# A new list of operations for a gated recurrence followed by a highway layer

## The chip, the cores and the metric

The kernel runs on one core of one Trainium2 chip. The metric is device microseconds of one execution. Of three runs of the kernel before, the median is 208.43 us (207.93 to 208.6).

One core has five engines with instruction streams of their own: TensorE (PE, matrix products and transposes; its weight loads are shown as PEld), VectorE (DVE), ScalarE (ACT), GpSimd (POOL) and SyncE (SP, which here issues the DMA transfers). Each works through its stream in order; between engines semaphores make an instruction wait for its data or for a buffer.

## The reference, cut to what matters

```python
# x, f_logit: [4, 6336, 256] float32; lower_bound: [256]; w_h, w_t: [256, 256]; b_t: [256]
sig = 1.0 / (1.0 + np.exp(-f_logit))
f = lower_bound + (1.0 - lower_bound) * sig
i = 1.0 - f
h = np.zeros((B, D))
for t in range(S):                      # a recurrence along the 6336 tokens of each sequence
    h = f[:, t] * h + i[:, t] * x[:, t]
    y[:, t] = h

y = y.reshape(B * S, D)                 # 25344 tokens of 256 channels
H = np.maximum(y @ w_h, 0.0)
T = 1.0 / (1.0 + np.exp(-(y @ w_t + b_t)))
out = T * H + (1.0 - T) * y             # float32
```

## The kernel before, in words

The 25344 tokens are cut into 28 units, numbered 0 to 27: two of 256 tokens, one of 512, twenty-three of 1024, one of 512 and one of 256. The recurrence runs along the tokens, so for it the data are turned: channels on the 128 partitions, in two halves (h = 0 and 1), tokens along the free axis.

A unit goes through these operations. The letter is the name in the list; the number behind it is the unit, and what stands behind the dot is the half or the piece.

| name | engine | what it does | line |
|---|---|---|---|
| l, x | SP | load of f_logit and of x for the unit (1 MB each for 1024 tokens) | L244 |
| u | ACT | u = sigmoid(-f_logit) | L256 |
| b | POOL, or DVE with a "v" | bv = u * x, in pieces of 512 tokens | L264 |
| i | PE | transposes of u, one half, into a PSUM bank (slots 0 and 1: a0, a1) | L271 |
| f | ACT, or DVE with a "v" | f = 1 + ncc * uT, one half | L282, L280 |
| p | PE | transposes of bv, one half, into a0 or a1 | L291 |
| s | DVE | the recurrence itself, a scan along the tokens, one half | L308 |
| z, g | PE | products of y with w_t and with w_h, for one half of the outputs | L320, L114 |
| t | ACT | t = sigmoid(z + b_t) | L333 |
| d | DVE | d = max(g, ncc * y), which with the folded weights is relu(y w_h) - y | L337 |
| e | POOL, or DVE with a "v" | d = d * t, in pieces | L343 |
| o | PE | back to tokens on partitions, and y + d added up in PSUM | L365, L366 |
| c | ACT, or DVE with a "v" | copy of o from PSUM to SBUF | L378, L376 |
| w | SP | store | L382 |

y is kept without the factor (1 - lower_bound), which is folded into the weights (WT, WH) and into the diagonal matrix that o uses (dg). cc and ncc are that factor and its negative. They come from lower_bound, transposed on PE by pc; pb and cb do the same for b_t. wt and wh load the weights. The token k is not part of the computation: k*3 puts three matmuls of zeros on PE, into the PSUM slot named behind it.

The order of everything is a list written out by hand or by a planner, one token for each operation, run from left to right (`for token in order.split()`). Each token issues its instructions, and every instruction is pinned (`tc.keep_in_program_order`), so the list fixes the order on each engine's stream. SP's stream too: a store whose copy isn't done holds back the loads behind it, and a load waits until the buffer that it names is free. The number behind the colon is the buffer: l and x have six slots each (0 to 5), u, f, bv and o four; z, g and o share three PSUM slots of two banks (0, 1, 2), and i and p two of one bank (a0, a1), which at the start and the end other operations use as well.

One more rule stands in the code (`shared`): a product on POOL (b, e) waits for the last product on DVE, or for the last of WT, WH and dg, that stands ahead of it in the list.

Of the kernel before, what the change touches and what calls it, by code (L numbers as in the profile page):

```python
# [53 lines left out]
e1.1 e1.0 k*2:0 w0.0 u4:1 z2.0:1 f3.0:1 z2.1:0 b4.0:1 s3.1:0 p3.0:0 o1.0:2 t2.1:0 u27:0 b4.1 c1.0:1 s3.0 w1.0 x8:3
i4.0:1 g2.0:0 f4.0:0 d2.0 i4.1:1 p4.0:0 l9:1 x9:4 l11:4 t2.0 u5:2 e2.1v e2.0v z3.0:0 g3.1:1 b27.0:0 z3.1:2 s4.0:1
p4.1:0 f4.1:1 i5.0:1 t3.0:0 t3.1 d3.1:1 b5.0:2 g3.0:0 f5.0:0 s4.1 o2.0:1 u6:1 b5.1 c2.0:2 d3.0 w2.0 i5.1:1 x11:0 e3.2
g4.1:2 p5.0:0 d4.1:0 b6.0:1 f5.1:1 s5.0:2 z4.1:0 t4.1:1 p5.1:1 b6.1 u7:2 e3.1 s5.1 l10:0 z4.0:1 t4.0 g4.0:0 i6.0:0
e3.0v p6.0:1 d4.0 o3.0:1 e4.2 b7.0:2 f6.0:0 s6.0:3 e4.0v i6.1:0 b7.1 u8:3 f6.1:1 o3.1:0 c3.0:0 c3.1:1 w3.1 w3.0 g5.0:2
p6.1:0 i8.1:1 z5.0:1 f8.1:0 x10:1 e4.1 t5.0:0 g5.1:0 i7.1:1 b8.0:1 s6.1 i7.0:0 d5.0:1 z5.1:1 l12:2 f7.1:1 p7.1:1 d5.1
f7.0:2 t5.1 b8.1 g6.0:2 p7.0:0 e5.1 k*3:0 o4.1:1 s7.1:0 z6.0:0 d6.0:2 s7.0 u9:1 b9.0:2 g6.1:2 c4.1:3 d6.1 i9.0:1  # L60
t6.0:1 b9.1 o4.0:1 u11:2 i9.1:0 f9.0v:1 c4.0:2 w4.0 e6.0v f9.1:2 g7.1:0 z6.1:2 k*3:1 e5.2v i8.0:1 z7.0:1 e5.0v t6.1
w4.1 f8.0:3 p8.1:0 d7.1:0 t7.0:0 g7.0:2 e6.1 p8.0:1 b11.0:3 o5.0:0 u10:1 c5.0:0 w5.0 x12:2 o5.1:1 c5.1:1 w5.1 s8.1:1
i11.1:0 z7.1:0 f11.1:0 s8.0 b11.1 l13:0 d7.0 p9.0:1 i10.1:0 z8.0:1 e6.2 b10.1:1 g8.1:2 t7.1 f10.1:3 p9.1:0 s9.0:2
o6.1:0 x13:0 i10.0:1 d8.1:1 s9.1 g8.0:2 t8.0:1 u12:3 o6.0:1 f10.0:1 c6.1:0 c6.0:2 b10.0 e7.0 i11.0:1 w6.0 p10.0:0 w6.1
f11.0:2 z8.1:0 t8.1 z9.0:1 t9.0:0 d8.0 g9.0:2 s10.0:3 i12.0:1 p10.1:0 l14:1 f12.0:1 d9.0:2 o7.0:0 g9.1:1 c7.0:1 x14:1
w7.0 s10.1 u13:1 o7.1:2 c7.1:3 w7.1 b12.0:2 l17:0 p11.0:1 d9.1 s11.0:0 z9.1:0 t9.1 i12.1:0 b12.1 l15:2 z10.1:1 g10.1:2
e8.0 t10.1:2 e9.0v b13.0:1 z10.0:0 f12.1:2 p11.1:1 b13.1 t10.0 o8.1:1 d10.1:0 p12.1:0 c8.1:0 o8.0:2 s11.1 u14:2
g10.0:0 d10.0 c8.0:2 b14.1:3 i13.1:1 e10.0 f13.1:0 g11.1:1 b14.0 z11.1:0 s12.1:1 d11.1:1 w8.0 t11.1:0 x15:0 w8.1
z11.0:2 i13.0:1 p12.0:0 s12.0 o9.0:0 t11.0 f13.0:2 g11.0:1 d11.0 o9.1:2 e11.0 p13.0:1 c9.0:1 u17:1 i14.0:0 f14.0v:1
c9.1:3 g12.0:0 u15:3 d12.0:2 b15.1:2 w9.0 z12.1:1 i17.0:0 f17.0:3 t12.1:1 o10.0:2 s13.0:2 o10.1:0 p13.1:0 c10.0:0  # L70
s13.1 b15.0 c10.1:1 i14.1:1 g12.1:1 z12.0:2 g13.0:0 i15.0:0 l16:1 f14.1:2 d12.1 p14.0:1 x16:2 d13.0:0 t12.0 o11.0:1
w9.1 g13.1:2 s14.0:3 f15.0:0 p14.1:0 o11.1:0 e12.0 w10.0 w10.1 i15.1:1 c11.0:2 u16:2 x17:1 b16.1:1 b16.0 z13.0:1 d13.1
f15.1:1 c11.1:0 z13.1:2 s14.1 t13.1:0 l18:0 t13.0 w11.0 p15.0:1 o12.1:0 i16.0:0 g14.1:2 s15.0:0 d14.1:1 e13.0 o12.0:1
p15.1:1 s15.1 c12.1:1 b17.1:2 f16.0:2 z14.1:0 z14.0:2 p16.0:0 s16.0:1 c12.0:3 t14.1:1 t14.0 g14.0:1 d14.0 i16.1:1
w11.1 l19:1 u18:3 x18:0 b17.0 e14.0 g15.1:0 d15.1:2 z15.0:2 i17.1:0 x19:3 f16.1:0 b18.0:3 p16.1:1 f17.1:1 b18.1 l20:2
s16.1 o13.1:1 t15.0:0 p17.0:0 g15.0:0 w12.1 d15.0 c13.1:0 u19:1 b19.1:1 o13.0:2 p17.1:1 z15.1:1 c13.0:2 z16.0:0
s17.1:2 t15.1 t16.0:1 z16.1:2 s17.0 g16.0:1 w13.1 t16.1 i18.0:1 d16.0:0 g16.1:0 o14.0:2 i18.1:0 f18.0:0 d16.1 e15.0v
o14.1:1 p18.0:1 s18.0:3 u20:2 w12.0 z17.0:0 c14.0:0 c14.1:1 f18.1:1 g17.0:2 d17.0:1 z17.1:1 b19.0 t17.0:0 i19.1:0
f19.1:0 p18.1:1 o15.1:0 w13.0 s18.1 t17.1 x20:1 i19.0:0 l21:0 g17.1:2 e16.0 d17.1 o15.0:1 f19.0:2 b20.0:2 b20.1
p19.1:0 x21:2 w14.0 i20.1:1 c15.1:2 g18.1:0 w14.1 s19.1:0 c15.0:3 z18.0:1 f20.1:1 l22:1 o16.0:2 d18.1:2 w15.1 u21:1  # L80
t18.0:1 p19.0:0 c16.0:0 i20.0:1 g18.0:0 s19.0 f20.0:0 o16.1:1 c16.1:1 z18.1:2 i21.1:0 b21.1:1 p20.0:1 t18.1 e17.0v
d18.0 o17.0:1 w15.0 z19.1:0 b21.0 f21.1:2 g19.0:2 s20.0:1 x22:0 d19.0:0 p20.1:0 s20.1 c17.0:2 t19.1:0 o17.1:1 u22:2
e18.0 z19.0:0 g19.1:2 b22.1:2 c17.1:3 t19.0 i21.0:1 d19.1 e19.0 i22.0:0 b22.0 f21.0:0 g20.1:1 z20.1:0 l23:2 w16.0
f22.0v:1 d20.1:1 w16.1 w17.0 x23:1 p21.1:1 w17.1 l24:0 u23:1 b23.0:3 t20.1:1 o18.0:2 o18.1:1 c18.0:0 s21.1:2 c18.1:1
p21.0:0 z20.0:0 b23.1 g20.0:2 i22.1:1 x24:2 t20.0 s21.0 f22.1:2 o19.1:1 p22.1:0 d20.0 c19.1:2 e20.0 i23.1:1 z21.0:0
g21.1:1 f23.1:0 t21.0:0 u24:2 p22.0:1 g21.0:2 b24.0:1 s22.1:3 i23.0:0 d21.1:2 f23.0:2 o19.0:0 z21.1:1 b24.1 s22.0
p23.1:0 d21.0 c19.0:3 t21.1 i24.0:1 w18.1 z22.0:0 z22.1:2 g22.1:1 s23.1:0 e21.0 w18.0 f24.0:1 w19.1 d22.1:0 l25:1
i24.1:1 x25:0 t22.0:1 t22.1 f24.1:0 e22.1 p23.0:0 o20.0:0 c20.0:0 w19.0 g22.0:1 p24.1:1 o20.1:2 u25:1 b25.0:2 s23.0
b25.1 p24.0:0 c20.1:1 d22.0 z23.0:0 s24.0:1 g23.0:1 t23.0:2 e22.0 l26:0 o21.0:2 c21.0:2 o21.1:0 s24.1 i25.1:0 g23.1:2
c21.1:3 x26:1 e22.2 g24.1:0 d23.0:1 f25.1:1 u26:2 b26.0:1 i27.1:1 i25.0:0 f27.1:0 d23.1 w20.0 z23.1:1 p25.0:1 f25.0:2  # L90
d24.1:2 s25.0:2 z24.0:2 p25.1:0 b26.1 t23.1 o22.0:0 e23.1 o22.1:1 t24.0:0 e23.2 z24.1:2 c22.0:0 s25.1 w20.1 g24.0:0
d24.0 e23.0v w21.0 c22.1:1 t24.1 w21.1 e24.0 w22.0 i26.0:1 e24.1 z25.0:1 i27.0:0 f26.0:2 g25.0:2 e24.2 i26.1:1 d25.0:0
# [330 lines left out]
```

## Time and profile before

| | |
|---|---|
| runs | 208.6, 207.93, 208.43 us |
| profiled execution, span from first to last instruction | 206.1 us |
| busy: PE, DVE, ACT, POOL | 192.6, 194.5, 191.9, 173.8 us |
| DMA, mean over the span | 78.68 MB, 382 GB/s |
| granted TensorE clock, mean | 0.995 |
| DVE waiting, longest | 4.4 us for the first load of x |
| SP waiting for copies of ACT ahead of stores | 110.2 us, 37 times |

Busy time is the union of an engine's instructions; the span counts from the first instruction of the program to the last, and a run takes 2 us more than it. PE's busy time counts matmuls in a pipeline and doesn't say that PE works at its peak.

### The profile page before, as it was taken

What the parts mean: (1) busy time and instruction counts of PE and PEld (TensorE: products, weight loads), DVE (VectorE), ACT (ScalarE), POOL (GpSimd) and SP (SyncE); (2) the same over time, 40 slices, a digit from 0 to 9 for tenths busy, and PEclk for the clock granted to TensorE, in tenths of its full rate; (3) what the DMA queues carried; (4) which work ended last, traced back from release to release, by engine and by line L of the source; (5) the groups of instructions that cost most, each with busy time, mean ns of one, the idle gap of its engine ahead of it and who ended that gap; (6) DMA issues with size and microseconds to landing.
All of it is one profiled execution on the core that took longest, in us unless ns stands there. A gap on an engine that the chain in (4) does not pass through costs nothing.

```text
span 206.1 us, 4635 instructions
## 1 busy us (share of the span) xinstructions
PE 192.6 (93%) x1837; PEld 133.8 (65%) x1837; DVE 194.5 (94%) x159; ACT 191.9 (93%) x192; POOL 173.8 (84%) x93
## 2 busy tenths in 40 slices
...
GB/s 196 370 424 422 411 418 423 409 423 417 414 423 408 429 417 426 423 420 413 425 424 416 433 411 417 429 415 418 407 422 422 414 392 378 286 104 204 138 382 248
DMA packets 16125, 78.68 MB, mean 382 GB/s; under 512 B 1764, under 2 KB 2536, under 8 KB 10216
## 3 DMA queue, kind: packets, MB, share of 16 engines
...
q8 instruction: 14, 0.23, 0.4%
...
q10 hardware_dynamic: 8, 0.00, 0.0%
...
## 4 chain that ended last, share of the span: by engine, by line
PE 53%; ACT 14%; DMA 13%; DVE 10%; issue 6%; POOL 2%; SPq 1%; ACTq 0%; DVEq 0%; POOLq 0%
DMA x<-in_x_dram 9%; DVE y L308 8%; PE op L366 7%; PE bT L291 7%; PE op L365 7%; PE g L320 7%; PE z L320 6%; PE uT L271 6%; PE g L114 6%; PE z L114 6%; ACT o L378 4%; ACT f L282 4%; DMA out_dram<-o 4%; ACT t L333 3%; POOL bv L264 2%
## 5 line engine op out<-in xcount | busy, mean ns | idle before, releaser
L264 POOL TENSOR_TENSOR bv<-u,x 128x1024 bf16<-128x1024 f16 (+1 forms) x49 | 100.9, 2085 | 16.9 <-DVE bt L207 10.7
L308 DVE TENSOR_TENSOR_SCAN y<-f,y,bT 128x1024 bf16<-128x1024 f16 (+5 forms) x54 | 106.8, 1989 | 0.2 <-PE bT L291 0.2
L343 POOL TENSOR_TENSOR d<-d,t 128x512 bf16<-128x512 bf16 (+3 forms) x33 | 73.3, 2234 | 9.6 <-DVE d L343 4.2
L337 DVE SCALAR_TENSOR_TENSOR d<-y,ncc,g 128x1024 bf16<-128x1024 bf16 (+2 forms) x56 | 63.1, 1137 | 1.5 <-PE g L320 1.0
L333 ACT ACTIVATE t<-z,bt 128x1024 bf16<-128x1024 f32 (+2 forms) x56 | 58.9, 1088 | 1.3 <-PE z L114 0.7
L282 ACT ACTIVATE f<-uT,ncc 128x1024 f16<-128x1024 f16 (+2 forms) x51 | 55.4, 1098 | 3.4 <-PE uT L271 2.2
L378 ACT COPY o<-op 128x1024 f32<-128x1024 f32 (+2 forms) x55 | 52.1, 984 | 2.4 <-PE op L366 1.6
L256 ACT ACTIVATE u<-l 128x2048 f16<-128x2048 f32 (+2 forms) x28 | 49.8, 1781 | 2.8 <-DMA l<-in_f_logit_dram 2.7
L366 PE MATMUL op<-ident_b,d 128*128 128x128 bf16 x396 | 49.5, 219 | 0.6 <-DVE d L343 0.6
L365 PE MATMUL op<-diag,y 128*128 128x128 f16 x396 | 49.7, 219 | 0.1
L366 PEld LDWEIGHTS <-d 128*128 128x128 bf16 x396 | 44.0, 113 | 3.2 <-DVE d L343 0.7
L365 PEld LDWEIGHTS <-y 128*128 128x128 bf16 x396 | 44.2, 113 | 1.7
L320 PE MATMUL g<-y,w_sb 128*128 128x512 bf16 (+1 forms) x112 | 39.5, 367 | 0.9 <-DVE d L337 0.7
L320 PE MATMUL z<-y,w_sb 128*128 128x512 bf16 (+1 forms) x112 | 39.3, 367 | 0.4 <-ACT o L378 0.4
L291 PE MATMUL bT<-ident_f,bv 128*128 128x128 f32 x198 | 31.8, 277 | 4.3 <-DVE y L308 2.6
L114 PE MATMUL z<-y,w_sb 128*128 128x512 bf16 x92 | 34.9, 379 | 0.0
L114 PE MATMUL g<-y,w_sb 128*128 128x512 bf16 x92 | 34.9, 379 | 0.0
L320 PEld LDWEIGHTS <-w_sb 128*128 128x128 f16 x224 | 21.6, 98 | 17.5 <-issue 0.9
L271 PEld LDWEIGHTS <-u 128*128 128x128 f16 x396 | 26.3, 98 | 10.2 <-issue 2.6
L271 PE MATMUL uT<-ident_h,u 128*128 128x128 f16 x396 | 31.2, 220 | 1.6 <-DVE y L308 0.8
L291 PEld LDWEIGHTS bT<-ident_f,bv 128*128 128x128 f32 x198 | 22.4, 141 | 12.3 <-ACT f L282 3.0
L114 PEld LDWEIGHTS <-w_sb 128*128 128x128 f16 x184 | 18.0, 98 | 16.7 <-issue 1.8
...
## 6 DMA issues: line engine op xcount, KB each, us to landing
...
l<-in_f_logit_dram SPq DMA_DIRECT2D x23, 1024.0 KB, 12.0
...
```

What stands on the lines that cost most here:

```text
L114: return pe.add_instruction(mybir.InstMatmult(name=nc.get_next_instruction_name(), start_tensor_calc=start, stop_tensor_calc=stop, tile_si ...
L264: shared(pin(e.tensor_mul(st[n]["bv"][:, a:c].rearrange("p k d j -> p k j d"), st[n]["u"][:, 2 * a:2 * c].rearrange("p (k j) d -> p k j d" ...
L271: pin(nc.tensor.transpose(uT[:, j * P:(j + 1) * P], st[n]["u"][:, j, h * P:(h + 1) * P], ident_h))
L282: pin(nc.scalar.activation(to, of, AF.Identity, scale=ncc[:, h:h + 1], bias=1.0))
L291: pin(nc.tensor.transpose(words[:, k:k + g * (P - 1) + 1:g], pair, ident_f))
L308: pin(nc.vector.tensor_tensor_scan(y[:, c:e], st[n]["f", h][:, c:e], st[n]["bT", h][:, c:e], 0.0 if fresh else carry[h], op0=ALU.mult, op1 ...
L320: pin(nc.tensor.matmul(p[:, a:e], w, half(n, "y", ki)[:, a:e], start=ki == 0, stop=ki == NH - 1))
L333: pin(nc.scalar.activation(half(n, "t", m), st[n]["z", m][:, :tokens(n)], AF.Sigmoid, bias=bt[:, m:m + 1]))
L337: pin(nc.vector.scalar_tensor_tensor(half(n, "d", m), half(n, "y", m), ncc[:, m:m + 1], st[n]["g", m][:, :tokens(n)], op0=ALU.mult, op1=AL ...
L343: shared(pin(e.tensor_mul(st[n]["d"][:, a:c], st[n]["d"][:, a:c], st[n]["t"][:, a:c])), not eng)
L365: pin(nc.tensor.matmul(o, half(n, "y", h)[:, cols], diag[:, h], start=True, stop=False))
L366: pin(nc.tensor.matmul(o, half(n, "d", h)[:, cols], ident_b, start=False, stop=True))
```

## The change

The list is replaced. Units, sizes of the pieces, buffers and the code of every operation stay as they are, word for word; the new file is two lines shorter, so its line numbers are lower by two behind the list. The new list has 822 tokens instead of 821.

What differs beside the order: which slot an operation names; which of the operations that can run on two engines run on DVE; and the idle matmuls' places. On DVE stand (b, e, f, c with a "v")

- before: b0.0 b1.0 b2.1 b3.1, e0.0 e2.1 e2.0 e3.0 e4.0 e6.0 e5.2 e5.0 e9.0 e15.0 e17.0 e23.0 e25.0 e25.2 e26.1 e27.1, f0.0 f1.1 f9.0 f14.0 f22.0, c25.1 c27.0
- after: b0.0 b1.0 b2.1 b3.0 b4.1, e1.0 e1.1 e0.0 e0.1 e2.1 e2.0 e3.2 e4.1 e5.2 e6.0 e6.2 e9.0 e15.0 e17.0 e23.1 e24.1 e25.2 e26.1 e27.1, f9.0 f14.0 f22.0, c25.0 c26.1 c27.0

The order on SP, at the start and in two later places:

```
before: l1 l0 x0 x1 l2 wt wh x2 l3 x3 l4 x4 l27 l5 x27 x5 l6 x6 l7 l8 x7 w0.0 w1.0 x8 l9 x9 l11 ...
after:  l0 x0 l1 wh l2 x1 x2 wt l3 x3 l4 l5 x4 x5 l6 l7 x6 l9 x9 x7 l8 w1.0 x8 w3.1 l10 w0.0 x10 ...
before: ... w6.0 w6.1 l14 x14 w7.0 w7.1 l17 l15 ... w11.0 w11.1 l19 x18 x19 l20 w12.1 w13.1 w12.0 w13.0 x20 ...
after:  ... x12 x14 w7.0 l14 w6.0 w6.1 l17 ... w12.0 l19 l27 w12.1 x27 w11.0 x18 x19 w10.0 w13.0 l20 ...
```

The diff, its first and last lines:

```diff
     order = """
-l1:0 l0:1 x0:0 x1:1 k*3:a0 l2:2 wt wh x2:2 l3:3 x3:3 l4:4 pc:0 x4:4 u0:0 l27:1 l5:5 b0.0v:0 x27:0 x5:5 u1:1 cc l6:0
-k*3:1 i0.1:0 f0.1:0 dg i1.0:1 b1.0v:1 f1.0:1 k*3:1 k*3:a0 p0.1:1 s0.1:0 i0.0:0 u2:0 f0.0v:0 p0.0:1 s0.0 x6:1 l7:2
-k*3:a0 WT pb:0 k*3:a1 i2.0:0 p1.0:1 f2.0:0 WH k*3:1 s1.0:1 i2.1:0 b2.1v:0 g0.0:1 b2.0 i1.1:1 z0.1:2 f2.1:1 cb f1.1v:2
-z0.0:0 g0.1:a0 p1.1:1 t0.0:0 d0.0:0 k*3:1 d0.1 p2.0:0 s1.1 k*3:0 e0.0v z1.1:1 p2.1:1 t0.1 u3:0 l8:3 g1.1:0 x7:2 s2.0:2
...
-f27.0:1 t25.0:1 p26.0:0 f26.1:3 o23.0:0 g25.1:1 z25.1:2 p26.1:1 s26.0:3 d25.1 c23.0:0 s26.1 w22.1 o23.1:0 p27.0:0
-t25.1 w23.0 c23.1:1 o24.0:1 e25.0v o24.3:2 s27.0:0 g26.0:a1 o24.2:0 c24.0:2 o24.1:1 d26.0:1 c24.3:0 c24.2 c24.1
-p27.1:0 e25.1 e25.2v z26.0:2 o25.0:0 o25.1:1 z26.1:a1 s27.1 g26.1:a0 t26.0:0 z27.0:2 c25.0:3 t26.1 c25.1v o25.2:0
-t27.0:1 o25.3:1 d26.1 g27.0:a0 w23.1 z27.1:a1 w24.1 w24.0 e26.0 c25.2:0 e26.1v o26.0:2 o26.1:0 d27.0:0 g27.1:a0 d27.1
-w25.0 c25.3 t27.1 e27.0 e27.1v o27.0:1 c27.0v:1 c26.0:2 o27.1:a0 c26.1 w25.1 w26.0 w27.0 c27.1:3 w27.1
+l0:0 pc:0 u0:0 i0.1:0 x0:0 cc i0.0:1 l1:1 wh b0.0v:0 f0.0:0 l2:2 dg pb:1 f0.1:1 k*3:a1 p0.0:0 x1:1 p0.1:1 s0.0:0 s0.1 k*3:2
+u1:1 k*2:0 k*3:a0 x2:2 i1.1:1 WH wt cb l3:3 f1.1:2 i1.0:0 g0.1:a1 x3:3 d0.1:0 g0.0:2 u2:2 b1.0v:1 f1.0:3 i2.0:1 k*3:a0 f2.0:0
+b2.1v:2 i2.1:0 p1.0:1 WT l4:4 d0.0 l5:5 z0.0:0 f2.1:1 s1.0:1 p1.1:0 s1.1 x4:4 z0.1:1 t0.0:0 b2.0 t0.1 p2.1:1 s2.1:2 g1.0:2
+u3:3 x5:5 d1.0:1 z1.1:0 k*3:1 p2.0:0 g1.1:1 z1.0:2 s2.0 l6:0 t1.0:1 b3.1:3 l7:1 i3.0:1 i3.1:0 t1.1 d1.1 f3.0:3 g2.1:2 b3.0v
...
+f27.0:1 z25.1:0 p26.1:0 o23.1:2 c23.0:2 t25.1 s26.0:2 s26.1 o24.0:1 c23.1:3 p27.0:1 c24.0:1 o24.3:0 g26.0:a0 e25.0 o24.2:2
+c24.3:0 w23.0 s27.0:3 o24.1:1 e25.2v d26.0:2 g26.1:a1 p27.1:0 c24.2 w23.1 e25.1 z26.0:0 d26.1 c24.1 t26.0:2 o25.1:2 s27.1
+c25.1:2 o25.0:1 e26.0 c25.0v z26.1:a1 w24.1 t26.1 o25.3:0 e26.1v c25.3:3 g27.0:a0 o25.2:2 z27.0:1 w24.0 w25.0 c25.2 d27.0:1
+z27.1:a1 o26.1:0 o26.0:2 g27.1:a0 t27.0:1 c26.1v:0 e27.0 d27.1 t27.1 e27.1v w25.1 o27.1:a1 c26.0 o27.0:1 c27.1:1 w26.0
+c27.0v:2 w27.1 w27.0
 """
```

More of the change, by code (lines that the diff above doesn't have):

```diff
@@ L54 @@
[L54 to L92, printed above, removed]
-f27.0:1 t25.0:1 p26.0:0 f26.1:3 o23.0:0 g25.1:1 z25.1:2 p26.1:1 s26.0:3 d25.1 c23.0:0 s26.1 w22.1 o23.1:0 p27.0:0
```

39 lines of the change are left out of this document (38 added, 1 removed).

## The prediction

> **What bounds the kernel now.** I read the stretches of time first, because an average over the span hides stages. Columns: stretch, its length, busy time of each engine with instructions, granted TensorE clock, DMA share, GB/s.
>
> ```profile
> core 0 of [0], span 206.1 us
> ...
> 0.00:20.00 20.00, 17.00 (x105) 9.28 (x106) 14.40 (x32) 12.37 (x17) 5.74 (x15) 1.00 0.92 350
> 20.00:60.00 40.00, 36.84 (x328) 24.43 (x326) 40.00 (x31) 39.97 (x38) 35.43 (x22) 1.00 1.02 418
> 60.00:120.00 60.00, 57.77 (x587) 41.74 (x585) 59.43 (x39) 59.58 (x55) 58.58 (x24) 1.00 1.02 420
> 120.00:190.00 70.00, 69.37 (x687) 49.24 (x686) 70.00 (x45) 69.30 (x68) 67.00 (x30) 1.00 0.91 368
> 190.00:206.10 16.10, 11.63 (x143) 9.10 (x140) 10.66 (x16) 10.68 (x18) 7.01 (x6) 0.94 0.63 246
> ```
>
> The third busy column is VectorE (DVE). From 20 to 190 us it is idle 0.57 us of 170. All its other idle time lies in the opening (20 - 14.40 = 5.60) and in the last 16 us (16.10 - 10.66 = 5.44). So the span is DVE's work, 194.49 us, plus 11.61 us of idle time in those three places, and a new order can only change these four numbers. ScalarE (ACT) is as full (0.03, 0.42 and 0.70 idle), POOL nearly, and the DMA engines have a share of about 1 up to 170 us: whatever makes one of these late reaches DVE soon.
>
> The opening, from the timeline (start, us, instruction, idle time before it and who ended it) and two pieces of the chain that ended last:
>
> ```profile
> 0.86 0.27 DVE L150 MEMSET zeros<- 128x256 uint32 x1 [0.86 <-PEq L407]
> ...
> 1.19 1.46 PE L153 MATMUL idle<-zeros 128*128 128x512 bf16 x3 [1.19 <-DVE zeros L150]
> ...
> 2.87 1.06 PE L114 MATMUL idle<-zeros 128*128 128x512 bf16 x2
> ...
> 3.86 0.26 PE L194 MATMUL lbT<-ident_f,lb 2*128 2x2 f32 x1
> ...
> 4.12 1.15 ACT L256 ACTIVATE u<-l 128x512 f16<-128x512 f32 x2 [1.27 <-DMA l<-in_f_logit_dram]
> ...
> 5.52 0.73 DVE L264 TENSOR_TENSOR bv<-u,x 128x512 bf16<-128x512 f16 x1 [4.39 <-DMA x<-in_x_dram]
> ...
> 6.11 0.60 PE L114 MATMUL idle<-zeros 128*128 128x512 bf16 x2
> ...
> 6.15 0.14 DVE L200 TENSOR_SCALAR ncc<-lbT 128x2 f32<-128x2 f32 x1
> ```
>
> ```profile
> 1.63 3.79 DMA x<-in_x_dram
> ...
> 6.82 14.43 DMA x<-in_x_dram
> ```
>
> DVE stands 4.39 us at b0.0v for x0, although lbT, on which the constants behind it wait, has been there since 3.86 + 0.26 = 4.12. x0 is the third transfer (issued 1.63, landed 5.42); x4, with 6.82 MB issued up to it against x0's 0.79, landed at 21.25, so 2.6 us per MB: loads land in order of issue, by bytes.
>
> The end, from the timeline and the last pieces of the chain:
>
> ```profile
> 196.39 0.73 DVE L308 TENSOR_TENSOR_SCAN y<-f,y,bT 128x256 bf16<-128x256 f16 x1
> ...
> 200.24 0.67 POOL L343 TENSOR_TENSOR d<-d,t 128x256 bf16<-128x256 bf16 x1 [1.79 <-DVE d L337]
> 200.25 1.08 ACT L378 COPY o<-op 128x512 f32<-128x512 f32 x2
> 200.87 0.48 DVE L337 SCALAR_TENSOR_TENSOR d<-y,ncc,g 128x256 bf16<-128x256 bf16 x1 [0.78 <-PE g L320]
> ...
> 202.07 0.43 DVE L376 COPY o<-op 128x256 f32<-128x256 f32 x1 [0.32 <-PE op L366]
> ```
>
> ```profile
> 200.62 0.23 PE g L320 x2
> ...
> 202.63 0.37 ACT o L378
> ```
>
> After the last scan starts (196.39, call it S) ACT's last copy ends 6.6 us later (203.00), and the end comes 3.1 us after that (the stores). In that stretch DVE's d27.1 waits 0.78 for its g, which stands on PE behind o26.0 and o26.1, and ACT copies both o26 halves (1.08).
>
> **The change, part by part.** Only the list differs. Prices are means by form (columns: count, then busy us and mean ns).
>
> ```profile
> L264 DVE TENSOR_TENSOR bv<-u,x 128x1024 bf16<-128x1024 f16 x1 | 1.8, 1753 | 0.0
> L376 DVE COPY o<-op 128x512 f32<-128x512 f32 x1 | 0.7, 692 | 0.2 <-PE op L366 0.2
> L343 DVE TENSOR_TENSOR d<-d,t 128x1024 bf16<-128x1024 bf16 x6 | 4.5, 756 | 0.0
> L343 DVE TENSOR_TENSOR d<-d,t 128x512 bf16<-128x512 bf16 x5 | 2.0, 420 | 0.1
> L343 DVE TENSOR_TENSOR d<-d,t 128x256 bf16<-128x256 bf16 x2 | 0.6, 278 | 0.1
> L280 DVE TENSOR_SCALAR f<-uT,ncc 128x256 f16<-128x256 f16 x2 | 1.0, 476 | 0.1
> L282 ACT ACTIVATE f<-uT,ncc 128x256 f16<-128x256 f16 x4 | 1.8, 473 | 1.4 <-DVE cc L201 1.1 <-PE uT L271 0.3
> L378 ACT COPY o<-op 128x512 f32<-128x512 f32 x11 | 6.0, 592 | 0.0
> L264 POOL TENSOR_TENSOR bv<-u,x 128x1024 bf16<-128x1024 f16 x45 | 96.2, 2165 | 5.4 <-DVE d L343 3.0 <-PE bT L291 1.3 <-DMA x<-in_x_dram 0.9
> L264 POOL TENSOR_TENSOR bv<-u,x 128x512 bf16<-128x512 f16 x4 | 4.7, 1192 | 11.5 <-DVE bt L207 10.7 <-DVE d L343 0.8
> L343 POOL TENSOR_TENSOR d<-d,t 128x1024 bf16<-128x1024 bf16 x2 | 4.3, 2155 | 0.7 <-DVE d L343 0.7
> L343 POOL TENSOR_TENSOR d<-d,t 128x512 bf16<-128x512 bf16 x15 | 17.4, 1172 | 4.8 <-DVE d L343 2.6 <-ACT t L333 1.1 <-ACT f L282 1.1
> L343 POOL TENSOR_TENSOR d<-d,t 128x256 bf16<-128x256 bf16 x4 | 2.6, 672 | 4.0 <-DVE d L337 1.8 <-DVE bv L264 1.3 <-DVE d L343 0.9
> ```
>
> *Work per engine.* Counting the two lists, DVE gets one b of 1024 (+1.75) and one copy of 512 (+0.69), gives up five e of 1024 (-3.78), gets five e of 512 (+2.10) and three of 256 (+0.83), and gives up two f of 256 (-0.95): **+0.65 us**, on the path. It could be +0.45, since these means add up to more than DVE's busy time (neighbours overlap by some hundredths), or +0.9 if new neighbours overlap less. ACT: two f of 256 less one copy, +0.35. POOL: -2.17 + 5 x 2.155 - 5 x 1.172 - 3 x 0.672 = +0.73. ACT and POOL are not on the path while DVE has work; their cover is ACT's gain at the start (below) and POOL's 4.57 + 1.42 + 3.00 = 9.0 us idle from 20 to 190. Idle matmuls on PE: 38 before (eleven k*3, one k*2, three in p3.1) and 38 after (twelve k*3, one k*2): nothing.
>
> *Opening.* cc now stands ahead of b0.0v, and l0 and x0 are the first two transfers. In the trace l0, second in the queue, released u0 at 4.12, so x0 in that place lands near 4.1 and u0 runs from some 3.5. DVE: ncc and cc at 4.12 to 4.45, b0.0v to 5.17, dg to about 6.0. Its idle time before that is 4.12 - 0.27 = 3.85 (the memset took 0.27), against 0.86 + 4.39 = 5.25. Then come waits that the old list didn't have. s0.0 needs p0.0, behind three idle matmuls that reuse the buffer of uT0.0, free after f0.0 (cc at 4.45, transposes, then 0.47: about 5.35); at the pace of the 6.11 row (0.22 each) PE reaches p0.0 near 6.1, s0.0 starts near 6.5: 0.5 us. d0.1 stands right behind WH and cb, and its g can only begin when WH is done: two matmuls, 0.23 in the 200.62 row, and a hand-over each way as long as the 0.3 of the 202.07 row: 0.5 us. b2.1v needs x2, at 2.36 MB instead of 2.62; by 2.6 us per MB it lands at 9.5, about 10.5 with the lower rate at the start, and b2.1v is reached at 10.3: 0.2. So 3.85 + 1.2 + 0.2 for small ones = 5.25 us of idle time in place of 5.60: **-0.35**. Bounds: -0.9 if the two hand-overs are hidden; +2.0 if PE goes at half pace there (first rival).
>
> *Loads and stores.* Same bytes; l27 and x27 go from the opening to the middle, w0 from ahead of x8 to behind l10, l9 and x9 ahead of x7 and l8. x4 is at 7.86 MB instead of 6.82 and lands 2.7 us later, near 24; its first reader b4.0 waits on POOL, and DVE reaches b4.1v only after s3.0, s3.1 and d2.0, at about 25. That stall is hidden by 1 us; without that cover DVE would pay what is over. I take 0, bounds 0 and +1.
>
> *The middle.* The old order leaves 0.57 us of DVE idle time. In the new one f and b stand further ahead of the scans that read them; e9.0v, e15.0v, e17.0v stay. I take 0.2 left: **-0.4**; it cannot win more than 0.57, and may lose 1 if PE comes late at several d.
>
> *The end.* d26.1 moves ahead of the last scan, c26.1 goes from ACT to DVE, and o27.1 (ACT) comes before o27.0 (DVE). From S: PE z26.0, two o25 parts, z26.1 (about 0.45 each) 1.8; t26.1 to 2.6; e26.1v to 2.95; o26.1 to 3.5 and o26.0 to 3.95; g27.1 4.2; d27.1 to 4.7; e27.1v to 5.0; o27.1 and o27.0 to 5.3; both copies side by side to 5.75. The old end needed 6.6, its last two copies one after the other. DVE's work behind S is about the same (c26.1 in, d26.1 out), so this is idle time: **-0.8**. Bounds -1.5 and +0.4 (c26.1 waits for POOL's e26.0 with d27.1 behind it on DVE, and e27.1v and the last store behind that).
>
> Sum: +0.65 - 0.35 - 0.4 - 0.8 = -0.9, a span near 205.2. Runs take 208.43 in the median, 2.3 more than the profiled span; I keep these 2.3: **207.6** (rounded up by 0.1).
>
> **The rivals.**
>
> *PE starts at half pace (slower).* In the old list PE is kept busy from 1.19 on: two idle matmuls took 1.06 at 2.87 and 0.60 at 6.11, so its pace doubled in between. The new list has no idle matmuls ahead of pc, and from 2.65 to 5.35 only two small transposes of constants and four of u. If the doubling comes as long after 5.35 as it came after the first matmul (4.9), the three idle matmuls ahead of p0.0 cost 0.6 more and the eight ahead of i1.1 and g0.1 up to 1.7 more; less what x2 would have cost anyway, 1 to 2 on DVE. With 1.6: -0.9 + 1.6 = +0.7, 209.1. It decides once the doubling comes after about 8 us. For it: the two rows; against: the clock column says 1.00 throughout, and some of the eight would run fast. The Trainium skill, "TensorE: Matmul & The Clock Gate", section "Part 1: The HAM clock gate", says that the array's clock is halved until one window of about 3.4 us has been busy, and that windows run freely. The two rows agree; by its figure an estimate of the release is between 8.8 and 12.2 us, and the time 208.7 to 209.6.
>
> *The load queue runs dry (slower).* Stores wait on SP for their copies, and loads behind them wait too:
>
> ```profile
> SPq L382 <- ACT o L378: 110.2, 37, 7.5
> ```
>
> ```profile
> 76.79 3.06 SPq L382 DMA_DIRECT2D out_dram<-o  x2
> ```
>
> ```profile
> 84.14 2.09 ACT L256 ACTIVATE u<-l 128x2048 f16<-128x2048 f32 x1
> ```
>
> The row at 76.79 is w7.0 and w7.1, issued when c7.0 was done; l14 stood ahead of them, and u14 read it at 84.14. Now l14 stands behind w7.0: issued at 77 to 78 it lands, with 1.6 MB of earlier loads and stores to come, about 5 us later, 1 to 2 us before its use. Likewise w5.0 ahead of l13, w12.0 and w12.1 ahead of l19 and x18, w13.0 ahead of l20. It decides if copies come over 2 us late; then each such place adds up to a microsecond: +1.5 to +3, so 209.0 to 210.5. For it: the 110.2 us; against: late copies also mean late use.
>
> *The end doesn't shorten (no change).* From e6.1 on POOL has two b of 1024, one of 512 and two e of 1024 more, three e of 512 less: +6.3 us, as it does less early. If it reaches e26.0 about 1 us late, the -0.8 is gone: 208.4. Against: 9.0 us of idle time.
>
> **How the numbers follow.** Forecast 0.42 (207.6, own range 206.5 to 208.2); half pace 0.25 (209.1); dry queue 0.18 (209.7); no shorter end 0.15 (208.4). A change under 0.3% (0.6 us, 207.8 to 209.1 counts as none) can't be told from none. Faster: most of the forecast's, 0.40 and 0.02 of the last. Same: 0.20 (last case, edges). Slower: 0.38. Range 206.3 to 210.2: the forecast's bounds down, the dry queue's up.
>
> **What would show it.** Right: DVE's first product near 4.5, idle 0 to 20 near 5.3, under 0.3 from 20 to 190, last ACT copy within 6 us of the last scan's start. Half pace: idle matmuls at 0.43 beyond 7 us and DVE waiting over 1 us at d for g. Dry queue: GB/s under 400 in a slice between 60 and 150, u or bv waiting for DMA. Wrong altogether: DVE idle over 1.5 us between 20 and 190.

## The result, and the profile after

The changed kernel takes 220.46 us in the median of four runs (219.7 to 222.71), the kernel before 208.32 (207.93 to 208.6): a ratio of 1.0605, interval 1.0569 to 1.0641, some 12 us slower. The forecast was 207.6 with a range up to 210.2, and the slower rivals reached 210.5. The sum failed by over 10 us. (Medians and ratios below leave out disturbed executions, two of four in two kernels and two of ten in a third, and each ratio is to executions of the kernel before that ran beside them, so it need not be the quotient of the medians shown.)

The profiled execution took 220.24 us with a span of 218.4. The same stretches as in the prediction (third busy column: DVE):

```profile
0.00:20.00 20.00, 14.98 (x85) 7.64 (x86) 13.81 (x30) 12.84 (x20) 4.93 (x13) 1.00 0.90 341
20.00:60.00 40.00, 36.69 (x327) 24.52 (x328) 39.90 (x33) 38.49 (x35) 31.32 (x17) 1.00 1.01 413
60.00:120.00 60.00, 55.05 (x543) 38.81 (x542) 57.61 (x38) 55.01 (x50) 55.48 (x22) 1.00 0.95 356
120.00:190.00 70.00, 65.13 (x645) 46.03 (x643) 66.18 (x41) 64.96 (x61) 66.52 (x26) 1.00 1.00 384
190.00:218.40 28.40, 23.79 (x247) 16.85 (x244) 23.46 (x25) 21.71 (x31) 20.18 (x14) 1.00 0.63 249
sum 218.40, PE 195.63 PEld 133.85 DVE 200.97 ACT 193.00 POOL 178.44; mean PE 39.13 PEld 26.77 DVE 40.19 ACT 38.60 POOL 35.69
```

Set against the forecast's four numbers:

| | forecast | after | difference |
|---|---|---|---|
| DVE busy | 194.49 + 0.65 = 195.14 | 200.97 | +5.8 |
| DVE idle, 0 to 20 us | 5.25 | 20 - 13.81 = 6.19 | +0.9 |
| DVE idle, 20 to 190 us | 0.2 | 0.10 + 2.39 + 3.82 = 6.31 | +6.1 |
| DVE idle, end | 5.44 - 0.8 = 4.64 | 28.40 - 23.46 = 4.94 | +0.3 |
| span | 205.2 | 218.4 | +13.1 |

Two terms of some 6 us each are new: DVE *works* longer, and it idles in the middle. The first is seen in the groups by form (count, then busy us and mean ns of one):

```profile
L341 DVE TENSOR_TENSOR d<-d,t 128x512 bf16<-128x512 bf16 x10 | 6.7, 682 | 0.6 <-ACT t L331 0.5
L341 DVE TENSOR_TENSOR d<-d,t 128x2048 bf16<-128x2048 bf16 x3 | 5.9, 1966 | 0.0
...
L262 DVE TENSOR_TENSOR bv<-u,x 128x1024 bf16<-128x1024 f16 x2 | 3.7, 1842 | 0.0
...
L341 DVE TENSOR_TENSOR d<-d,t 128x1024 bf16<-128x1024 bf16 x1 | 1.3, 1316 | 0.0
L341 DVE TENSOR_TENSOR d<-d,t 128x256 bf16<-128x256 bf16 x5 | 1.3, 285 | 0.1
```

The same product of 512 columns takes 682 ns in the mean instead of 420, that of 1024 takes 1316 instead of 756, that of 2048 takes 1966 instead of 1295. DVE's timeline beside POOL's, at two places (start, us, instruction, idle time before it):

```profile
64.45 1.32 DVE L341 TENSOR_TENSOR d<-d,t 128x1024 bf16<-128x1024 bf16 x1
65.69 1.27 DVE L335 SCALAR_TENSOR_TENSOR d<-y,ncc,g 128x1024 bf16<-128x1024 bf16 x1
66.88 1.18 DVE L341 TENSOR_TENSOR d<-d,t 128x512 bf16<-128x512 bf16 x1
...
83.95 2.47 DVE L341 TENSOR_TENSOR d<-d,t 128x2048 bf16<-128x2048 bf16 x1
```

```profile
58.82 8.96 POOL L262 TENSOR_TENSOR bv<-u,x 128x1024 bf16<-128x1024 f16 x4
...
83.20 7.38 POOL L262 TENSOR_TENSOR bv<-u,x 128x1024 bf16<-128x1024 f16 x3 [2.62 <-DMA x<-in_x_dram]
```

These are e6.0v, e6.2v and e9.0v, and each starts while POOL is in the middle of a run of its own products. POOL's rows are long too: three products in 7.38 us, where its mean of 2165 ns makes 6.5. The d between them, with one operand in PSUM, keeps its 1.27.

The second term is seen in the chain that ended last, between 64 and 92 us:

```profile
64.45 1.32 DVE d L341
...
66.96 1.10 DVE d L341
68.06 2.27 DVE y L306
...
80.83 0.91 ACT o L376
81.76 0.34 SPq L380
82.15 9.67 DMA l<-in_f_logit_dram
91.85 1.80 ACT u L254
```

Both stretched products stand in it. Then come ACT's copies, the last of them c7.0; the store w7.0 that waited for it (SPq L380); behind that the load l14, 9.67 us until it landed; and u14, at 91.85 where it had started at 84.14 before. SP's waits for ACT's copies, the waits for loads and for stores' landings, and the transfer rate over 40 slices of the span:

```profile
SPq L380 <- ACT o L376: 127.5, 28, 11.0
```

```profile
POOL bv L262 <- DMA x<-in_x_dram: 14.0, 6, 5.4
...
ACT u L254 <- DMA l<-in_f_logit_dram: 4.4, 5, 3.2
ACT o L376 <- DMA out_dram<-o: 4.0, 3, 2.3
```

```profile
GB/s 204 340 425 420 416 422 416 415 418 423 383 308 203 359 428 326 371 424 425 374 414 292 327 364 347 386 395 338 420 422 427 414 399 371 383 297 137 155 334 290
```

The longest wait of SP grew from 7.5 to 11.0 us, the b's wait for x from 0.9 to 14.0 (8.2 of it before 25 us), and the rate, 418 to 420 from 20 to 120 us before, falls to 308 and 203 between 60 and 71 us (a slice is 5.46 us), and to 326, 292, 327 and 347 in four more slices up to 136.

### The profile page after: what moved, and what is told of

Same layout as the page of the kernel before. It is cut to its first block, busy times and chain, and to the rows that moved or that the text cites. A ratio compares the mean times of both kernels' runs of the same rounds, so it can differ in the third digit from the quotient of the medians.

```text
span 218.4 us, 4627 instructions
## 1 busy us (share of the span) xinstructions
PE 195.6 (90%) x1837; PEld 133.8 (61%) x1837; DVE 201.0 (92%) x162; ACT 193.0 (88%) x193; POOL 178.4 (82%) x89
## 4 chain that ended last, share of the span: by engine, by line
PE 30%; DVE 23%; DMA 17%; ACT 14%; issue 9%; POOL 4%; SPq 1%; ACTq 0%; DVEq 0%; POOLq 0%
DVE y L306 13%; DMA l<-in_f_logit_dram 10%; DMA out_dram<-o 7%; DVE d L335 6%; ACT o L376 5%; PE g L318 4%; PE z L318 4%; PE op L364 4%; ACT t L331 4%; PE op L363 4%; PE bT L289 4%; PE z L112 3%; PE uT L269 3%; ACT u L254 3%; DVE d L341 3%
## 5 line engine op out<-in xcount | busy, mean ns | idle before, releaser
L341 POOL TENSOR_TENSOR d<-d,t 128x2048 bf16<-128x2048 bf16 (+3 forms) x30 | 76.2, 2548 | 6.1 <-DVE d L341 2.6
L280 ACT ACTIVATE f<-uT,ncc 128x1024 f16<-128x1024 f16 (+2 forms) x53 | 54.3, 1036 | 6.4 <-PE uT L269 6.0
L331 ACT ACTIVATE t<-z,bt 128x1024 bf16<-128x1024 f32 (+2 forms) x56 | 57.3, 1052 | 2.1 <-PE z L112 0.8
L376 ACT COPY o<-op 128x1024 f32<-128x1024 f32 (+2 forms) x54 | 50.0, 946 | 8.1 <-DMA out_dram<-o 4.0
L254 ACT ACTIVATE u<-l 128x2048 f16<-128x2048 f32 (+2 forms) x28 | 48.7, 1738 | 4.4 <-DMA l<-in_f_logit_dram 4.4
```

Source lines behind the costliest of these rows:

```text
L331: pin(nc.scalar.activation(half(n, "t", m), st[n]["z", m][:, :tokens(n)], AF.Sigmoid, bias=bt[:, m:m + 1]))
L341: shared(pin(e.tensor_mul(st[n]["d"][:, a:c], st[n]["d"][:, a:c], st[n]["t"][:, a:c])), not eng)
L376: pin(nc.scalar.copy(to, of))
```

## The experiments

Theory A: loads stand behind stores on SP, the stores wait for late copies, the queue of transfers runs short and the loads come late. Theory B: the copies wait for the landing of the store that used the same o buffer. Theory C: the new order of the computing costs the time. Theory D came with the run without stores; it is a cause inside the order of the computing, so C's ranges leave room for it.

**Buffers, and loads first.** The new list with five o buffers; then, besides, each load ahead of up to three stores:

```diff
-x11:5 ... w4.0 ... w5.0 l13:1 ... w3.0 ... w5.1 ... x13:0 x12:2 x14:3 ... w7.0 l14:2 ... w6.0 w6.1 l17:3
+l12:0 x11:5 w0.0 w4.1 l13:1 w2.0 w4.0 x13:0 x12:2 x14:3 w5.0 l14:2 w3.0 w5.1 l17:3 w7.0
```

> The new list, with five buffers for the output copies (o) instead of four; nothing else. Theory A (the loads stand behind stores on SP, the queue gets shallow and the DMA engines lose pace): nothing gained at the root, 217 to 221 us, loads still ending some 13 us later than in the kernel before. Theory B (ACT's copies wait for the landing of the store that used the same o buffer: 4.0 us, longest 2.3): the wait is gone and with it what it drags along, 212 to 216 us. Theory C (the new order of the computing itself costs the time): 219 to 221 us.

> As the run with five o buffers, and on SP each load stands ahead of up to three of the stores that stood ahead of it; the order on PE, ACT, DVE and POOL is that of the new list. Theory A: 207 to 210 us, DMA back at 415 GB/s or more in all slices from 20 to 170 us, loads ending within 4 us of where they end in the kernel before. Theory B: no better than the run with five o buffers alone. Theory C: 216 to 221 us.

Five buffers: 221.78 us (220.99 to 223.09), 1.0597 (1.0507 to 1.0687). The wait of the copies for stores is gone and nothing is gained: B is out. Loads first: 218.92 us (217.35 and 220.49), 1.0463 (1.0335 to 1.0592), a miss for A. In the profiled execution (222.47 us) the rate stayed near 420 up to 75 us, but the stores now stood behind the loads, and the wait that the fifth buffer had removed came back, larger:

```profile
ACT o L375 <- DMA out_dram<-o: 6.0, 4, 2.9
```

The two queues of work hold each other: loads first makes buffers free late, stores first makes loads late. How much of the time that wait cost isn't settled: in the same profile e15.0v, a product of DVE, took 4.51 us beside POOL's, where it takes 1.24 alone (see below).

**One place of the queue, in the kernel before.** l14 and x14 go behind w7.0, which is one of the places that the prediction named. The edit does one thing more: x14 now stands ahead of l14, as it does in the new list.

```diff
-l14:1 ... x14:1
 w7.0
+x14:1 l14:1
```

> The list of the kernel before with two tokens moved: l14 and x14 stand behind w7.0 instead of ahead of w6.0, w6.1 and w7.0. Computing order untouched. Theory A: the queue gets shallow near 78 us, the DMA rate falls under 350 GB/s for some us, and the run is 1 to 4 us longer (209.5 to 212.5). The price that I gave in the forecast (up to 1 us for each such place): 208.3 to 209.3. Theory C: no change, 207.9 to 208.7.

211.61 us (210.81 to 212.55), 1.0116 (1.0048 to 1.0183): 2.4 us (1.0 to 3.8 by the interval) for two tokens on SP, where I had priced such a place at one at most. The megabyte of x14 ahead of l14 is in that price. The stretches around it:

```profile
82.00:86.00 4.00, 3.66 (x50) 3.00 (x48) 4.00 (x4) 2.34 (x3) 3.68 (x2) 1.00 0.97 327
86.00:90.00 4.00, 1.92 (x12) 0.82 (x10) 4.00 (x3) 2.83 (x3) 1.44 (x2) 1.00 1.04 435
90.00:94.00 4.00, 3.97 (x29) 3.28 (x29) 1.19 (x2) 4.00 (x4) 4.00 (x2) 0.62 0.96 365
```

The rate dips to 327, PE is busy only 1.92 of the 4 us behind it, and then its granted clock is 0.62 (the column behind the five engines). The Trainium skill, "TensorE: Matmul & The Clock Gate", section "Part 1: The HAM clock gate", says that an idle window of about 3.4 us sends the array's clock back to half; here the clock fell after a lull of only 2.11 us in a row, and in the profile after none fell after one of 2.63 us (from 92.12 on), so the length of a lull alone doesn't decide. Nor is the dip needed for the 2.4 us: the two executions with mean clocks of 0.999 and 1.000 took 210.81 and 211.87. In the profile after no dip stands in the middle (1.00 in every stretch above); the other three executions of the changed kernel had mean clocks of 0.983 to 0.992 and took 219.7 to 222.71 us, against 220.24 without a dip, so dips don't make the 12 us.

**All loads a little later, in the kernel before.**

```diff
-x8 l9 x9 ... w5.0 x12 w5.1 ... w6.1 l14 x14 w7.0 ... w8.0 x15 w8.1
+l9 x9 x8 ... w5.0 w5.1 x12 ... w6.1 w7.0 l14 x14 ... w8.0 w8.1 x15
-l16 x16 w9.1 w10.0 w10.1 x17 l18 w11.0 w11.1 l19 x18 x19 l20 w12.1
+l16 w9.1 w10.0 w10.1 x16 l18 w11.0 x17 w11.1 l19 x18 w12.1 x19 l20
```

> The list of the kernel before with the loads from x8 on moved later on SP, by at most one scan's place: x8 behind x9, x12 behind w5.1, l14 and x14 behind w7.0, x15 behind w8.1, x16 behind w10.1, x17 and l18 behind w11.0, x19 and l20 behind w12.1. Computing order untouched. Theory A with the loss of pace that follows each place where the queue gets short: 210.5 to 214 us, each dip costing more than the time for which the queue is empty. If only an empty queue costs: 208.2 to 209.2, as every load still lands ahead of its use at a constant 415 GB/s.

214.49 us (211.71 to 214.68), 1.0254 (1.0182 to 1.0327): about 6 us in the median, with nothing moved but loads. Not all of that is the queue. b4.1 came later on POOL, and e2.1v, which starts while it runs, took 1.63 us instead of 0.44. And the profiled execution (214.68) has two dips of the clock, 0.70 and 0.58 in the 4 us from 28 and from 126 on; three executions with mean clocks of 0.980 to 0.987 took 214.34 to 214.68, the one at 0.995 took 211.71, 3.3 more than the kernel before. That the dips make the rest is likely, not shown.

**Depth of the queue, by itself.**

> No computing at all, the output is left mostly unwritten: only transfers of the kernel's shapes. 14 loads of 1 MB for each of the depths 6, 4, 3, 2 and 1 (a load waits until the load so many places ahead has landed and DVE has copied one column), then loads of 1 MB with one or two stores of 0.5 MB after each, at depths 4, 3, 2, 1. Theory A needs: about 420 GB/s at depth 6, and already at depth 3 or 2 a fall below 350 GB/s with packets of more than 400 ns. If only the latency of an issue counts: 420 GB/s at 6, 4 and 3 with packets of 309 ns throughout, and at 2 and 1 gaps between the transfers but no slow packets.

The stages of depth 6, 4, 3, 2, 1, and loads with stores at depth 4 (DVE, POOL, clock, DMA share, GB/s):

```profile
6.00:38.00 32.00, 1.85 (x12) 0.00 (x0) 1.00 1.00 419
```

```profile
43.00:75.00 32.00, 2.00 (x13) 0.00 (x0) 1.00 0.97 402
78.00:111.00 33.00, 1.91 (x13) 0.00 (x0) 1.00 0.99 407
114.00:150.00 36.00, 2.00 (x13) 0.00 (x0) 1.00 0.96 376
153.00:218.00 65.00, 2.01 (x13) 0.00 (x0) 1.00 0.57 208
225.00:268.00 43.00, 2.17 (x24) 0.00 (x0) 1.00 0.98 369
```

Loads alone keep their pace down to a depth of three, lose a tenth at two and half at one; so A's stronger form, a loss of pace at depth three, is wrong for loads. With stores between them the rate is 369, 347 and 356 at depths of four, three and two, so there the depth hardly matters. Of the single packets of 8192 bytes that start in these stretches, 5 of 1636 took over 400 ns at depth 6, 105 of 1654 at depth 2, 116 of 944 with stores; in the changed kernel it was 378 of 5900, against 61 of 5901 before. So a queue of two loads is slow as well as soon empty; which of the two costs the changed kernel its time isn't separated.

**Another order on SP, in the new list.** Most loads further ahead:

```diff
-x4 x5 l6 l7 x6 l9 x9 x7 l8 w1.0 x8 w3.1 l10 w0.0 x10 l11 w4.1 w2.0 l12 x11 w4.0 w5.0 l13
+x4 x7 x5 l6 l7 x6 l9 x8 x12 l11 w0.0 l8 w1.0 l13 w3.1 w2.0 l10 x9 x10 w4.1 w3.0 l12 w4.0
...
```

> The new list with another order on SP alone (from x4 on; most loads further ahead, stores of one unit closer together), and the buffer numbers of l, x and o that follow from it; four o buffers; on PE, ACT, DVE and POOL the same instructions in the same order as in the new list. Theory A (the order of loads and stores on SP empties the DMA queue): 207.5 to 211.5 us, loads ending within 5 us of the kernel before. Theory C (the new order of the computing costs the time): 216 to 221 us.

216.58 us (216.24 to 216.96), 1.04 (1.0377 to 1.0422): a third of the loss comes back, not the whole, outside A's range and inside C's. SP's order is one cause; either it isn't the only one, or this order isn't good enough.

**No stores.** Stores of units 4 to 18 left out of the new list, first in one execution, later in four:

> The new list without the stores of units 4 to 18 (30 stores, 15.7 MB of output are left out); all computing, all copies and all loads stay. No load stands behind a store there, and no copy waits for one. Theory A (and B): 205 to 208.5 us. Theory C: 215 us or more.

> The new list without the stores of units 4 to 18, as in the earlier single look (220.1 us, where one product of DVE, e15.0v, stood 7.4 us beside three products of POOL), now in several executions. If the two causes simply add: the queue's part is gone and the products' part left, 211 to 215 us in the median. If the products' cost is drawn anew in each execution: a spread of 4 us or more between executions, 212 to 221.

220.09, and 219.51 us (219.36 to 219.97), 1.0535 (1.05 to 1.0569): no load waits for a store, and the time is hardly better. A alone doesn't hold it, and neither branch of the second expectation came: the spread is 0.6 us, and it isn't 211 to 215. The trace of the first execution gave theory D. DVE, and POOL beside it:

```profile
129.74 7.44 DVE L339 TENSOR_TENSOR d<-d,t 128x2048 bf16<-128x2048 bf16 x1
```

```profile
127.63 8.47 POOL L260 TENSOR_TENSOR bv<-u,x 128x1024 bf16<-128x1024 f16 x4
```

e15.0v took 7.44 us (7.43 in the later profile); it ended 1.1 us, near the 1.24 that it takes alone (measured below), behind the last of POOL's four products in a row. Theory D: a product on DVE and one on POOL exclude each other. The later profile shows what comes behind it:

```profile
136.00:140.00 4.00, 0.09 (x1) 0.12 (x2) 4.00 (x3) 0.00 (x0) 0.42 (x1) 0.51 1.01 412
140.00:144.00 4.00, 4.00 (x17) 2.45 (x18) 3.28 (x2) 0.93 (x1) 2.90 (x1) 0.64 0.37 147
```

While DVE stood, PE, ACT and POOL ran out of work, and PE's clock fell to 0.51 and 0.64. The mean clock was 0.981 to 0.984 in all five executions. In the changed kernel itself e15.0v took 1.22 us; the longest product e on DVE there is e9.0v with 2.47.

**Products side by side, by themselves.**

> No loads and none of the kernel's result: single instructions of the kernel's shapes. POOL runs four products b (128x1024 f16) back to back, and DVE at the same time one product e (2048 or 512), started 0.4 to 1.3 us behind POOL's first by an operation d of 256 to 1024 columns; beforehand the products alone, and a round with only d and scans beside POOL. Theory D (a product on DVE and one on POOL exclude each other, both reading two operands from SBUF; which was first keeps the other waiting until it is done): alone 1.3 us for 2048 and 0.42 for 512; beside POOL longer by what is left of POOL's running product, 0.9 to 1.8 us, or by several of them; d and scan unchanged at 1.25 and 2.3. Theory A alone (transfers): all durations the same with and without POOL.

DVE's product of 2048 alone, twice (first row); beside POOL, started later and later behind POOL's first product; at last one of 512:

```profile
12.62 2.47 DVE L73 TENSOR_TENSOR d<-d,t 128x2048 bf16<-128x2048 bf16 x2
...
26.46 2.98 DVE L73 TENSOR_TENSOR d<-d,t 128x2048 bf16<-128x2048 bf16 x1
29.36 1.27 DVE L76 SCALAR_TENSOR_TENSOR q<-y,one,g 128x1024 bf16<-128x1024 bf16 x1
...
56.10 2.18 DVE L73 TENSOR_TENSOR d<-d,t 128x2048 bf16<-128x2048 bf16 x1
...
64.92 2.17 DVE L73 TENSOR_TENSOR d<-d,t 128x512 bf16<-128x512 bf16 x1
```

```profile
17.61 8.36 POOL L83 TENSOR_TENSOR bv<-u,x 128x1024 bf16<-128x1024 f16 x4 [17.17 <-DVE mark L90]
26.24 9.35 POOL L83 TENSOR_TENSOR bv<-u,x 128x1024 bf16<-128x1024 f16 x4 [0.27 <-DVE mark L90]
```

Alone it takes 1.24 us. Beside POOL it takes that and what is left of POOL's running product, 2.98 down to 2.18 us; POOL's four products take 9.35 instead of 8.36, as the next one waits for DVE's. The d (1.27) and the scan (2.28) are as long as ever. D holds for these rounds. The Trainium skill, "SBUF — State Buffer", section "Who interferes with whom", has the rule: a DVE instruction with two SBUF inputs contends with a GpSimd instruction that reads SBUF, and whichever issues first holds the port for the whole instruction. These rows agree. That a product of DVE waits out several of POOL's (the 7.44 us) happened in none of the rounds here, and stays unexplained.

**One such product, in the kernel before.** e15.0v a place earlier on DVE:

```diff
-d16.0:0 g16.1:0 o14.0:2 i18.1:0 f18.0:0 d16.1 e15.0v
+d16.0:0 e15.0v g16.1:0 o14.0:2 i18.1:0 f18.0:0 d16.1
```

> The list of the kernel before with one token moved: e15.0v, on DVE, stands directly behind d16.0 instead of behind d16.1. Same instructions, no wait added. There it falls into the middle of POOL's b19.1 instead of its last third of a microsecond. Theory D: e15.0v takes 2.6 to 2.9 us instead of 1.42, and the run is 0.8 to 1.6 us longer (209.2 to 210.0). Theory A: 208.2 to 208.7.

```profile
129.06 2.78 DVE L340 TENSOR_TENSOR d<-d,t 128x2048 bf16<-128x2048 bf16 x1
```

2.78 us, as D said, 1.36 more than before; the run takes 210.92 us (210.35 to 212.35), 1.0131 (1.0091 to 1.0172). That is 2.7 us, twice the stretch itself and more than the 0.8 to 1.6 expected. In the profiled execution (212.35) PE was busy only 1.65 of the 4 us from 130 on, and its clock was 0.57 in the next 4. The three executions with mean clocks of 0.993 to 0.996 took 210.35 to 210.42, 2.0 us more than the 208.34 of the kernel before, the three at 0.987 to 0.989 took 211.42 to 212.35. So a part beyond the stretch goes with such dips; that the rest is POOL's and its readers' delay is argued.

**Without the seven products, without both.** Seven DVE products are left out of the new list: six of those that were stretched in the profile after, and e15.0v. Seven of its own are left out of the old; then the new list without them and with the other order on SP, and without them and without the stores.

> The new list with seven products of DVE left out (e5.2v e6.0v e6.2v e9.0v e15.0v e17.0v e23.1v; 5.9 us by the means of the kernel before), to be set against the kernel before with its own seven left out. Theory D: 205 to 210 us, at most 5 us more than its counterpart, where the full kernels differ by 12.1. Theory A (only the queue): 214 to 218 us, 10 to 13 more than the counterpart.

> The list of the kernel before with its seven products of DVE in the middle left out (e6.0v e5.2v e5.0v e9.0v e15.0v e17.0v e23.0v; 6.6 us by their means). Both theories: 202 to 208 us.

> Both suspected causes taken away at once: the new list with the other order on SP and without the seven products of DVE that ran into POOL's (left out, as in the earlier run). If theories A and D together hold the loss: 205.5 to 210 us, within 3 us of the kernel before without its seven (207.3). If the computing order has a third cause of its own: 213 us or more.

> The new list without the stores of units 4 to 18 and without the seven products of DVE (both left out): the two causes taken away in another manner. A and D together: 204.5 to 208.5 us. A third cause in the computing order: 213 us or more. If only one of the two mattered, this would be no better than the run without stores (220.1) or the run without the products (220.8).

Medians in us, with the ratio to the full kernel before:

| new list | all products | seven products left out |
|---|---|---|
| as it is | 220.46, 1.0605 (1.0569 to 1.0641) | 218.30, 1.0476 (1.0408 to 1.0544) |
| other order on SP | 216.58, 1.04 (1.0377 to 1.0422) | 213.34, 1.0255 (1.0218 to 1.0291) |
| no stores, units 4 to 18 | 219.51, 1.0535 (1.05 to 1.0569) | 208.73, 1.002 (0.9995 to 1.0045) |
| old list | 208.32 | 207.27, 0.9954 (0.9928 to 0.998) |

Without the products, though 5.9 us of DVE's work by the old means are gone, the new list gains only 2.2 us, a miss for D's 205 to 210. The chain of the profiled execution shows two loads in it, l13 and l14, each behind a store:

```profile
66.83 0.34 SPq L379
67.22 9.92 DMA l<-in_f_logit_dram
...
82.99 0.34 SPq L379
83.38 9.13 DMA l<-in_f_logit_dram
```

That execution took 223.66 us and has two dips of the clock (0.62 and 0.57 in 4 us); the two that the median counts took 217.19 and 219.41 and were not profiled, so that loads hold them too is argued. Without the stores 1 us is gained, and e15.0v with what follows it costs most of what is left. That cell shows what a collision can cost, and not what the products cost in the changed kernel, where this one didn't happen.

Without both, the new list is at 208.73, 1.4 us above the old list without its seven. The two causes don't add: taking away either alone leaves most of the loss, taking away both leaves almost none. A large third cause in the order of the computing would show in that cell. The old list without stores wasn't run; but its ACT was idle only 0.03 + 0.42 + 0.70 = 1.15 us from 20 to 190, so I estimate that it has little more than that to gain, and that a third cause is at most some 3 us. The 213.34 of the other order on SP is what I had written down for a third cause, and it isn't settled. Two things are left in it: POOL's products wait 6.7 us for x, 4.56 of it for x4, and e24.1v still takes 1.71 us beside POOL's products instead of 0.42.

**The end alone.** The old list up to s23.0, the new one from there:

> The list of the kernel before up to s23.0, and from there the order of the new list (its end). My forecast's term for the end, -0.8 us: 207.2 to 208.0 us. The rival that the end doesn't shorten: 208.1 to 208.8 us. Last copy of ACT or DVE within 6 us of the last scan's start in the first case, 6.6 in the second.

208.62 us (208.37 to 210.14), 1.0023 (1.0003 to 1.0043). The time is the rival's (208.1 to 208.8). But the last copies end 203.56 - 197.85 = 5.7 us after the last scan starts, as the forecast said:

```profile
188.93 1.50 DVE L340 TENSOR_TENSOR d<-d,t 128x512 bf16<-128x512 bf16 x2
...
197.85 0.74 DVE L305 TENSOR_TENSOR_SCAN y<-f,y,bT 128x256 bf16<-128x256 f16 x1
...
203.14 0.42 DVE L373 COPY o<-op 128x256 f32<-128x256 f32 x1 [0.55 <-PE op L363]
```

But that scan starts 1.46 us later than in the old list, and part of it is again a product beside POOL's: e23.1v and its successor, both of 512, take 1.50 us instead of 0.84 (first row).

**The opening.** Three idle matmuls more, on the list without stores and products:

```diff
-l0:0 pc:0 u0:0 i0.1:0
+l0:0 pc:0 k*3:1 u0:0 i0.1:0
```

> The new list without the stores of units 4 to 18 and without the seven products of DVE (208.7 us, DVE idle 7.8 us in the first 20), and one token k*3:1 (three idle matmuls) added behind pc, so that PE works through the time in which it waited for l0. If PE's half pace until 10.2 us is what the opening costs: the idle matmuls run at 0.22 us each from about 6 to 8 us on, DVE idles 1 to 2.5 us less in the first 20, and the run takes 206.3 to 207.8. If not: 208.3 to 209.2.

208.99 us (207.91 to 209.38), 1.0021 (0.9996 to 1.0046), no gain. The edit didn't do what it was made for: PE's matmuls doubled their pace near 9.6 us, not at 6 to 8. Without the three it was near 10.5: of two idle matmuls from 9.76 on that took 0.97 us, against 1.06 for a pair wholly at half pace, only the last tenth was faster. So the price of the half pace stays open.

## Why the prediction was wrong, by its own steps

- **"Work per engine", +0.65 us on DVE: this step failed.** The count of the products was right. Their prices were the means of a list in which DVE's products, from 14 us on, began with POOL idle or in the last 0.6 us of its running product, and I took them as properties of the instruction; the worst I allowed was +0.9. In the new order b3.0v, e5.2v, e6.0v, e6.2v, e9.0v, e17.0v and e23.1v began inside a run of POOL's products. DVE's work grew by 6.48 us: the products e alone took 6.7 + 5.9 + 1.3 + 1.3 = 15.2 us, where the old means make 10.2. The one rule of the code that bears on this (`shared`) stood in my own description: it makes POOL wait for a product of DVE that stands ahead in the list, and nothing makes DVE wait for POOL. I used that rule as an order and not as a sign that the two exclude each other. No rival had it.
- **"The load queue runs dry": the mechanism and the places were right, the price was wrong.** w5.0 ahead of l13 and w7.0 ahead of l14 are where the rate falls first. I priced a place at up to a microsecond, +1.5 to +3 in all, chance 0.18. One place alone, with x14 ahead of l14, cost the old list 2.4 us, and loads a little later all along 3.3 to 6. What I held against it, "late copies also mean late use", is the wrong way round: copies, stores, loads, u and again copies are a ring, so that a delay comes back. The chain above shows one turn of it, from c7.0 by w7.0 and l14 to u14. My forecast that l14 would be issued at 77 to 78 took c7.0 from the old order; it was issued at 82.15 and landed 9.67 us later, not 5.
- **"Middle", -0.4 from 20 to 190 us: wrong by 6.1.** 6.31 us of idle time instead of 0.2, and the sum had nothing for the loads that come late. How much of it comes from loads and how much from stretched products isn't separated. I treated DVE's idle time as separate numbers, although from 120 to 190 us PE, DVE and ACT were each idle at most 0.7 us; with so little slack a delay on one of them soon reaches the others.
- **"Loads", 0: the landing was right, its cover was not.** I put x4's landing near 24 us, and b4.0 started on POOL when it was there:

```profile
24.08 2.14 POOL L262 TENSOR_TENSOR bv<-u,x 128x1024 bf16<-128x1024 f16 x1 [5.36 <-DMA x<-in_x_dram]
```

  I looked only at whether DVE would wait for x4. POOL lost 5.36 us there: up to 60 us it did 4.93 + 31.32 = 36.25 us of work, where it had done 5.74 + 35.43 = 41.17. That POOL was late by this when DVE's products came was argued from these numbers, not tested by itself.
- **"Opening", -0.35: +0.6 in this execution.** The first product started at 4.45 (4.5 forecast), but the wait for d0.1's g was 1.24 us and not 0.5:

```profile
10.20 0.48 DVE L335 SCALAR_TENSOR_TENSOR d<-y,ncc,g 128x256 bf16<-128x256 bf16 x1 [1.24 <-PE g L318]
```

  The first rival named the reason and its sign, a wait over 1 us at d behind idle matmuls at 0.43. What I held against it, the clock column's 1.00, is no evidence: the column says 1.00 from 2 to 4 us in the profile before as well, where two idle matmuls took 1.06 us, against 0.60 later. In this execution the pace doubled near 7.6 us. In eight profiles of seven other lists that open alike on PE it did so near 8.4 once and between 9.7 and 10.9 us seven times, with 7.0 to 8.0 us of DVE idle time in the first 20 us; the prediction's estimate from the Trainium skill, "TensorE: Matmul & The Clock Gate", section "Part 1: The HAM clock gate", 8.8 to 12.2, holds for those seven. The size of this term, 0.6 to 2.4 us above the old idle time, is near the 1 to 2 of that rival, and a small part of the 12.
- **"End", -0.8: right in itself.** The last copies end 215.58 - 209.88 = 5.7 us after the last scan starts, 6.6 before. The run with the end alone shows that it isn't a gain all the same, as the last scan comes later.

What I had written as "wrong altogether", DVE idle over 1.5 us between 20 and 190, is what came.
